# The second MoE in the order of the source on every queue, with z's sums on VectorE

## The chip, the core and the metric

The kernel runs on one core of a Trainium2 chip. The metric is the device time of one execution in microseconds (us), as the median of several runs. The engines are TensorE (PE; its weight loads are listed as PEld), VectorE (DVE), ScalarE (ACT), GpSimd (POOL) and SyncE (SP, which issues the DMAs here). The trace comes from one profiled execution.

## The reference, cut to what matters

```python
x = attention(q, k, v, mem_k, mem_v)      # 3072 tokens x 512, float32
h = np.maximum(x @ w_in, 0.0)             # first MoE: 512 -> 2048
x = (h * h) @ w_out                       # 2048 -> 512
g = x @ w_gate                            # second MoE: 512 -> 1536
val = x @ w_val
out = (g / (1 + np.exp(-g)) * val) @ w_out2    # 1536 -> 512
```

The second MoE takes gate and value as one 2x2 block product: the weights (A11, A12, A21, A22; 256 columns each) times the transposed tokens (B11, B21 of one block of 384 tokens, B12, B22 of the next), by a scheme with seven products in place of eight. It needs sums of the weights (S1 to S4, made once and kept in DRAM) and of the tokens: T1 = B12 - B11, T2 = B22 - B11, T3 = B22 - B12, T4 = T2 - B21. Every float32 factor is cut into a high part (a cast to float32r) and a low part (the rest), and a product is three passes over these parts.

## The kernel before, in words

Until 630 us of the profile the kernel does the attention and the first MoE. In the second MoE it takes the tokens in four groups `s` of two blocks and the 1536 columns in twelve slices `f`: 48 steps `i`, each with `gated(i)` (line 422) and then `output(i)` (line 463).

`gated` makes the seven products in two PSUM banks of `hbank`, p and q in turn, each with six matmuls (line 410: two halves of 128 rows, three passes). A product may start when the bank's last content, that of the product two earlier, has been read. The readers: ScalarE copies A11's product to p1 (line 426); VectorE adds S2's to p1 (u2, line 430), A12's to p1 (g0, line 434; ScalarE then takes its silu, line 435), S3's to u2 (u3, line 439), S1's to u3 and to u2 (c22 and u4, lines 443, 444), subtracts A22's from u3 (line 448) and multiplies by g0 (line 449), adds S4's to u4 (line 454); ScalarE takes u4's silu (line 455) and VectorE multiplies c22 by it (line 456). The two results are cut by `rounded` (line 416): ScalarE casts the high part uh (line 76), VectorE subtracts to get the low part ul (line 79).

`output(i)` is a generator of 18 matmuls of 512 columns from those parts into six banks, which sum over f. They run one step later, a few behind each product: `fill(1)`, `fill(3)` and so on. At the last f each bank is copied to a tile `o` by ScalarE or VectorE in turn and stored.

`side(1)` to `side(7)` stand behind the products and emit jobs for later steps: `load_gv` (a DMA of one half of a step's weights, 1024 or 768 columns, into one of the two tiles of "cut"), `split_gv` (ScalarE casts whi, POOL subtracts to get wlo, in two pieces), `load_out` and `split_out` (the same for the output weights of two steps), and for the next s, from f = 2 on, `load_z` (two DMAs of 768 KB, line 371), `split_b1`, `sums_1` and `sums_2` (the four T by POOL, lines 385 to 393) and `split_t` (ScalarE casts, VectorE subtracts, 128x768). Weights, output weights and the parts of the T share the 32 tiles of the pool `wp`.

What sets the order: TensorE follows the source from the second block of the first MoE on (`tc.manual_schedule`, line 560). The order of the other engines and of SP's DMAs is chosen at build time by a list scheduler, which goes by the order of the source as a priority and by when it takes data and buffers to be there. Each engine's queue is then worked off in that fixed order, so an instruction that waits holds up those behind it.

Of the kernel before, what the change touches and what calls it, by code (L numbers as in the profile page):

```python
# [7 lines left out]
F32 = mybir.dt.float32  # L8
# [3 lines left out]
ALU = mybir.AluOpType  # L12
# [17 lines left out]
NT2 = 384  # L30
# [17 lines left out]
def attention_moe_moe_kernel(ctx, tc, att, w1, w2, out):  # L48
# [9 lines left out]
    pe, act, dve, pool, sp = nc.tensor, nc.scalar, nc.vector, nc.gpsimd, nc.sync  # L58

    wp = ctx.enter_context(tc.tile_pool(name="wp", bufs=32))  # L60
# [13 lines left out]
    def split(hi, lo, src, hi_engine, lo_engine):  # L74
        if hi_engine is act:
            act.copy(hi, src)  # L76
        else:
            hi_engine.tensor_copy(hi, src)
        lo_engine.tensor_tensor(lo, src, hi.bitcast(F32), ALU.subtract)  # L79
# [150 lines left out]
    for t, n in enumerate(BLOCKS[1:], 1):  # L230
        for j in range(n):
            e = QB * (t - 1) + (j + 1) * QB // n - 15
# [4 lines left out]
    def attention(hs):  # L237
        for lag, fn, u in sorted(plan.pop(hs, []), key=lambda a: (-a[0], a[2])):
            fn(u)


    w = {}
# [3 lines left out]
    def pair(pool_, tag):  # L246
        return [pool_.tile([128, 1024], R, tag=tag, name=n) for n in ("whi", "wlo")]
# [61 lines left out]
    w2t = {}  # L309
# [24 lines left out]
        w["raw2", key] = raw[:, 0:n]  # L334
        sp.dma_start(out=raw[:, 0:n], in_=src)

    def split_w(key):
        raw = w.pop(("raw2", key))
        n = raw.shape[1]
        w2t[key] = pair(wp, "w")  # L340
        for c in (0, n // 2):
            split(*(t[:, c:c + n // 2] for t in w2t[key]), raw[:, c:c + n // 2], act, pool)

    def spare():
        return wp.tile([128, WC], F32, tag="w", name="spare")
# [5 lines left out]
        raw = rawp.tile([128, WC], F32, tag="cut", name="gvraw", bufs=CB)  # L351
        fetch((i, half), raw, w2g[seq2[i][1], :, c:c + NGV[half]], NGV[half])

    def split_gv(i, half):
        split_w((i, half))


    def load_out(i):
        fetch(("out", i), spare(), w2o[seq2[i][1] // 2], WC)

    def split_out(i):
        split_w(("out", i))

    zt, zraw = {}, {}

# [13 lines left out]
        hi, lo = zt[s][("B11", "B21")[k]] = [t[:, rows, 0:NT2] for t in zt[s]["x"]]  # L379
        split(hi, lo, zraw[s][0][:, rows], act, dve)  # L380

    def sums_1(s):
        z0, z1 = zraw[s]
        b11, b12, b22 = z0[:, 0:2], z1[:, 0:2], z1[:, 2:4]
        pool.tensor_tensor(b11, b12, b11, ALU.subtract)
        pool.tensor_tensor(b12, b22, b12, ALU.subtract)
        zt[s].update(T1=b11, T3=b12, B22=b22)

    def sums_2(s):
        z0, z1 = zraw[s]  # L390
        t2 = spare()[:, 0:2 * NT2].rearrange("p (k n) -> p k n", k=2)
        pool.tensor_tensor(t2, z1[:, 2:4], z0[:, 0:2], ALU.subtract)
        pool.tensor_tensor(z0[:, 2:4], t2, z0[:, 2:4], ALU.subtract)
        zt[s].update(T2=t2, T4=z0[:, 2:4])

    def split_t(s, name):
        src = zt[s][name]
# [3 lines left out]
    utile = {}  # L401

    def product(i, wname, zname, to):
        c = WAT[wname]
        whi, wlo = (t[:, c % WC:c % WC + QC] for t in w2t[i, c // WC])
        zh, zl = zt[seq2[i][0]][zname]
        n = 0
        for wt, z in ((whi, zh), (whi, zl), (wlo, zh)):
            for k in range(2):
                pe.matmul(to, wt[:, k * 128:k * 128 + 128], z[:, k], start=n == 0, stop=n == 5)  # L410
                n += 1

    def tmp():
        return up.tile([128, NT2], F32, tag="tmp", name="tmp", bufs=7)

    def rounded(u):
        uh = gp.tile([128, NTM], R, tag="gh", name="uh", bufs=3)[:, 0:NT2]
        ul = gp.tile([128, NTM], R, tag="gl", name="ul", bufs=3)[:, 0:NT2]
        split(uh, ul, u, act, dve)
        return uh, ul  # L420

    def gated(i, fill, side):
        p, q = (hbank[(7 * i + n) % 2][:, 0:NT2] for n in range(2))
        p1, u2, g0, u3, c22, u4 = (tmp() for _ in range(6))
        product(i, "A11", "B11", p)
        act.copy(p1, p)  # L426
        fill(1)
        side(1)
        product(i, "S2", "T2", q)
        dve.tensor_tensor(u2, q, p1, ALU.add)  # L430
        fill(3)
        side(2)
        product(i, "A12", "B21", p)
        dve.tensor_tensor(g0, p, p1, ALU.add)
        act.activation(g0, g0, AF.Silu)
        fill(3)
        side(3)
        product(i, "S3", "T3", q)
        dve.tensor_tensor(u3, q, u2, ALU.add)
        fill(3)  # L440
        side(4)
        product(i, "S1", "T1", p)
        dve.tensor_tensor(c22, p, u3, ALU.add)
        dve.tensor_tensor(u4, p, u2, ALU.add)
        fill(3)
        side(5)
        product(i, "A22", "T4", q)
        dve.tensor_tensor(u3, u3, q, ALU.subtract)
        dve.tensor_tensor(u3, u3, g0, ALU.mult)  # L449
        first = rounded(u3)  # L450
        fill(3)
        side(6)
        product(i, "S4", "B22", p)
        dve.tensor_tensor(u4, p, u4, ALU.add)  # L454
        act.activation(u4, u4, AF.Silu)
        dve.tensor_tensor(c22, c22, u4, ALU.mult)
        utile[i] = first, rounded(c22)
        fill(2)
        side(7)

    outs = [b[:, i] for i in range(2) for b in (yb0, yb1, abank)]

    def output(i):
        s, f = seq2[i]
        hi, lo = (t[:, f % 2 * DM:f % 2 * DM + DM] for t in w2t["out", i // 2 * 2])
        order = [(3 * b + j, p) for b in range(2) for p in range(3) for j in range(3)]
        if f == NF2 - 1:
            order = [(j, p) for j in range(6) for p in range(3)]
        for j, p in order:
            uh, ul = utile[i][j // 3]  # L470
            u, wt = ((uh, hi), (uh, lo), (ul, hi))[p]
            c = 128 * (j % 3)
            pe.matmul(outs[j], u[:, c:c + 128], wt, start=f == 0 and p == 0, stop=f == NF2 - 1 and p == 2)  # L473
            if f == NF2 - 1 and p == 2:
                o = up.tile([128, DM], F32, tag="o", name="o", bufs=3)
                if j % 2:
                    dve.tensor_copy(o, outs[j])
                else:
                    act.copy(o, outs[j])
                r0 = (6 * s + j) * 128  # L480
                sp.dma_start(out=out[r0:r0 + 128, :], in_=o)
            yield
# [16 lines left out]
    def at(hs, fn, *args):  # L499
        wplan.setdefault(hs, []).append((fn, args))  # L500
# [10 lines left out]
        at(a - 8, load2, c)  # L511
        at(a, prep2, c)
    for f, fn, *args in (
        (0, load_z, 0), (2, split_b1, 0, 0), (3, split_b1, 0, 1), (3, sums_1, 0), (4, sums_2, 0),
        (4, split_t, 0, "T2"), (5, split_t, 0, "T3"), (6, split_t, 0, "T1"), (6, load_gv, 0, 0), (7, split_t, 0, "T4"),
        (7, load_gv, 0, 1), (8, split_t, 0, "B22"), (9, load_out, 0), (9, split_gv, 0, 0), (10, split_gv, 0, 1),
        (11, load_gv, 1, 0), (12, split_out, 0), (12, load_gv, 1, 1), (13, split_gv, 1, 0), (14, split_gv, 1, 1),
        (14, load_out, 2),
    ):
        at(last + 4 * f + 2, fn, *args)  # L520
    lookahead = 2
# [2 lines left out]
    def side(hs):  # L524
        attention(hs)
        for fn, args in wplan.pop(hs, []):
            fn(*args)
# [29 lines left out]
    ordered = ExitStack()  # L557
# [22 lines left out]
    def job(i, slot, fn, *args):  # L580
        if i < len(seq2):
            jobs.setdefault((i, slot), []).append((fn, args))

    for i, (s, f) in enumerate(seq2):
        if i > 0:
            if i + 1 < len(seq2):
                job(i - 1, 4, load_gv, i + 1, 0)
                job(i - 1, 7, load_gv, i + 1, 1)
                job(i, 2, split_gv, i + 1, 0)
                job(i, 5, split_gv, i + 1, 1)  # L590
        if i % 2 == 0 and i + 2 < len(seq2):
            if i > 0:
                job(i, 7, load_out, i + 2)
            job(i + 1, 3, split_out, i + 2)
        if f == 0 and i + NF2 < len(seq2):
            for at_f, slot, fn, *args in (
                (2, 2, load_z), (4, 4, split_b1, 0), (5, 4, split_b1, 1), (6, 1, sums_1), (6, 4, sums_2),
                (7, 4, split_t, "T2"), (8, 4, split_t, "T3"), (9, 4, split_t, "T1"), (10, 4, split_t, "T4"),
                (11, 3, split_t, "B22"),
            ):  # L600
                job(i + at_f, slot, fn, s + 1, *args)
    todo = iter(())

    def fill(n):
        for _ in range(n):
            next(todo, None)

    for i in range(len(seq2)):
        def side2(slot):
            for fn, args in jobs.pop((i, slot), []):  # L610
                fn(*args)

        gated(i, fill, side2)
        todo = output(i)
    fill(18)
    ordered.close()
    uctx.close()
# [59 lines left out]
```

## Time and profile before

| | |
|---|---|
| median of 3 runs (lowest, highest) | 1245.71 us (1243.95, 1247.89) |
| the profiled execution, its span | 1246.47 us, 1244.7 us |
| TensorE busy in the span | 1168.9 us, 94% |
| VectorE, ScalarE, POOL busy | 718.2, 608.5, 376.1 us |
| second MoE, from its first product to its last matmul | 630.26 to 1240.39 us |

The span is that of the trace, from the first instruction to the last; the execution's own time is a little longer. TensorE is busy nearly all the time, so what can be gained without fewer matmuls is its idle time and the time in which its granted clock is low. In the rows, "idle before" names what ended an engine's wait, and "hbank L410" is a matmul of line 410.

### The profile page before, as it was taken

How to read it: one execution, taken by the hardware profiler on the slowest of the kernel's cores; microseconds unless marked ns; L12 is line 12 of the kernel's file. 1: busy time of each engine (PE TensorE's matmuls, PEld its weight loads, DVE VectorE, ACT ScalarE, POOL GpSimd, SP SyncE). 2: the span in 40 equal slices, each digit the busy share in tenths (PEclk: the TensorE clock that was granted, in tenths of full speed). 3: DMA queues.
4: the chain of work that ended last, by engine and by line, in shares of the span. 5: the costliest groups of instructions: out<-in, count | busy, mean ns of one | idle time of the engine just before them, and what ended most of it. 6: DMA issues, size and time to landing. Idle time of an engine off the chain costs nothing.

```text
span 1244.7 us, 20548 instructions
## 1 busy us (share of the span) xinstructions
PE 1168.9 (94%) x8000; PEld 1101.3 (88%) x8000; DVE 718.2 (58%) x1223; ACT 608.5 (49%) x1518; POOL 376.1 (30%) x313
## 2 busy tenths in 40 slices
PE   2699999999999999999989999899998999989998
PEld 1599999999999999999978999789987899878897
DVE  7997335546454464533356666566665666555654
ACT  5686545556455564545643344544344343443422
POOL 0000000202020020002565445754367543564610
PEclk9999999999999999999989999899999999989999
DMA  7553205527243451501353224522245232353301
GB/s 266 192 207 116 74 25 177 185 87 253 82 161 131 166 197 61 207 1 51 103 167 100 77 73 145 178 88 85 93 123 183 77 95 68 113 165 98 93 13 51
DMA packets 49441, 150.22 MB, mean 121 GB/s; under 512 B 4800, under 2 KB 14528, under 8 KB 44992
## 3 DMA queue, kind: packets, MB, share of 16 engines
q1 hardware_dynamic: 49344, 148.92, 36.0%
q8 instruction: 62, 1.02, 0.3%
q14 instruction: 35, 0.29, 0.1%
HBM read 122.16 MB, written 26.74 MB: 120 GB/s over the span
## 4 chain that ended last, share of the span: by engine, by line
PE 78%; DVE 8%; DMA 5%; POOL 3%; ACT 2%; issue 2%; SPq 0%; DVEq 0%; POOLq 0%; ACTq 0%
PE hbank L410 24%; PE yb L295 19%; PE hbank L264 19%; PE yb L473 9%; PE abank L473 4%; POOL wlo L79 3%; DMA wraw<-in_w_dram 3%; PE abank L197 2%; DMA gvraw<-w2g 2%; DVE pT L178 2%; PE abank L136 1%; DVE tmp L449 1%; DVE ul L79 1%; DVE cut L97 1%; ACT uh L76 1%
## 5 line engine op out<-in xcount | busy, mean ns | idle before, releaser
L79 POOL TENSOR_TENSOR wlo<-gvraw,whi 128x512 fp32r<-128x512 f32 x192 | 233.7, 1239 | 247.4 <-ACT whi L76 122.7
L264 PE MATMUL hbank<-x,whi 128*128 128x384 f32 x1024 | 200.3, 337 | 1.0 <-ACT x L76 0.6
L274 DVE TENSOR_TENSOR gl<-r,gh 128x384 fp32r<-128x384 f32 x128 | 79.2, 620 | 182.8 <-ACT r L273 182.3
L264 PEld LDWEIGHTS hbank<-x,whi 128*128 128x128 f32 x1024 | 180.4, 189 | 1.8 <-ACT x L76 0.9
L328 POOL TENSOR_TENSOR wraw<-cut 128x256 f32<-128x256 f32 x24 | 19.8, 847 | 462.6 <-DVE mx L149 343.8
L410 PE MATMUL hbank<-whi 128*128 128x384 f32 x480 | 126.5, 345 | 19.9 <-DVE tmp L454 13.8
L76 ACT CAST whi<-gvraw 128x512 fp32r<-128x512 f32 x192 | 100.5, 563 | 86.3 <-DMA gvraw<-w2g 38.6
L271 ACT ACTIVATE r<-hbank 128x384 f32<-128x384 f32 x128 | 62.9, 491 | 143.5 <-PE hbank L264 140.6
L410 PEld LDWEIGHTS hbank<-whi 128*128 128x128 f32 x480 | 89.2, 190 | 47.0 <-DVE tmp L454 20.0
L76 ACT CAST uh<-tmp 128x384 fp32r<-128x384 f32 x96 | 49.3, 514 | 161.7 <-DVE tmp L449 124.2
L410 PE MATMUL hbank<-wlo,whi 128*128 128x384 f32 x480 | 126.3, 344 | 0.0
L410 PE MATMUL hbank<-whi,wlo 128*128 128x384 f32 x480 | 124.7, 341 | 0.0
L295 PE MATMUL yb<-gh,whi 128*128 128x384 f32 x512 | 116.3, 341 | 0.0
L295 PE MATMUL yb<-gh,wlo 128*128 128x384 f32 x512 | 113.4, 335 | 0.0
L295 PE MATMUL yb<-gl,whi 128*128 128x384 f32 x512 | 113.3, 335 | 0.0
L264 PE MATMUL hbank<-x,wlo 128*128 128x384 f32 x512 | 109.8, 335 | 0.0
L79 DVE TENSOR_TENSOR ul<-tmp,uh 128x384 fp32r<-128x384 f32 x96 | 77.4, 806 | 48.2 <-ACT uh L76 46.0
L178 DVE STREAM_TRANSPOSE pT<-prob 32x256 f32<-32x256 f32 x224 | 97.3, 434 | 3.6
L410 PE MATMUL hbank<-z,whi 128*128 128x384 f32 x384 | 86.1, 347 | 5.8 <-ACT tmp L426 5.8
L295 PEld LDWEIGHTS yb<-gh,whi 128*128 128x128 f32 x512 | 89.2, 188 | 2.5
L295 PEld LDWEIGHTS yb<-gh,wlo 128*128 128x128 f32 x512 | 91.4, 188 | 0.0
L295 PEld LDWEIGHTS yb<-gl,whi 128*128 128x128 f32 x512 | 90.9, 188 | 0.1
(91 smaller groups left out, 2132.9 us busy)
## 6 DMA issues: line engine op xcount, KB each, us to landing
wraw<-in_w_dram SPq DMA_DIRECT2D x34, 1024.0 KB, 6.6
gvraw<-w2g SPq DMA_DIRECT2D x48, 512.0 KB, 3.5
gvraw<-w2g SPq DMA_DIRECT2D x48, 384.0 KB, 3.1
qk<-in_att_dram SPq DMA_DIRECT2D x32, 464.0 KB, 4.5
spare<-w2o SPq DMA_DIRECT2D x24, 512.0 KB, 3.3
v<-in_att_dram SPq DMA_DIRECT2D x32, 256.0 KB, 3.5
y1d<-ys SPq DMA_DIRECT2D x8, 768.0 KB, 3.8
w2g<-wraw SPq DMA_DIRECT2D x12, 512.0 KB, 4.0
```

What stands on the lines that cost most here:

```text
L76: act.copy(hi, src)
L79: lo_engine.tensor_tensor(lo, src, hi.bitcast(F32), ALU.subtract)
L97: dve.scalar_tensor_tensor(w.bitcast(I32), upper, 3, lower, ALU.logical_shift_left, ALU.bitwise_or)
L178: dve.transpose(pT[row:row + 32, :, 32 * c:32 * c + 32], probs[u % 2][32 * c:32 * c + 32, :, col:col + 32],)
L197: pe.matmul(o[r:r + D, h // NI, h % NI // 2], s["v"][:, h * D:(h + 1) * D], pT[:, h], start=True, stop=True, tile_position=(0, r),)
L264: pe.matmul(hps, wt[:, k * 128:(k + 1) * 128], x[:, k, 0:n], start=i == 0, stop=i == 3 * KD - 1)
L271: act.activation(r, hps, AF.Relu)
L274: dve.tensor_tensor(gl, r, gh.bitcast(F32), ALU.subtract)
L295: pe.matmul(y[e], wt[:, c:c + 128], g, start=f == 0 and p == 0, stop=f == NF1 - 1 and p == 2)
L328: pool.tensor_tensor(o, x, y, op)
L410: pe.matmul(to, wt[:, k * 128:k * 128 + 128], z[:, k], start=n == 0, stop=n == 5)
L473: pe.matmul(outs[j], u[:, c:c + 128], wt, start=f == 0 and p == 0, stop=f == NF2 - 1 and p == 2)
```

## The change

All engines and SP's DMA queue now follow the source in the second MoE, as TensorE did already, and the source is put in another order: behind each product its reader comes first, then `side`, then `fill`. The cut of u's halves is divided: `halves_of` emits the cast on ScalarE and `low_of` the subtraction on VectorE. The first half's subtraction comes behind u4's addition; the second half's cast comes at the end of the step and its subtraction behind the next step's u2 (`pending`). `split_gv` and `split_out` are divided into two parts with slots of their own. The four sums of z go from POOL to VectorE, one at a time.

```diff
+    def sum_t(s, name):
+        z0, z1 = zraw[s]
+        b11, b12, b21, b22 = z0[:, 0:2], z1[:, 0:2], z0[:, 2:4], z1[:, 2:4]
...
+        o, x, y = {"T1": (b11, b12, b11), "T3": (b12, b22, b12), "T2": (t2, b22, b11), "T4": (b21, t2, b21)}[name]
+        dve.tensor_tensor(o, x, y, ALU.subtract)
...
-    def rounded(u):
+    def halves_of(u):
...
-        split(uh, ul, u, act, dve)
+        act.copy(uh, u)
+        return uh, ul, u
+
+    def low_of(uh, ul, u):
+        dve.tensor_tensor(ul, u, uh.bitcast(F32), ALU.subtract)
         return uh, ul
+    pending = []
...
         product(i, "A11", "B11", p)
         act.copy(p1, p)
+        side(1)
         fill(1)
-        side(1)
         product(i, "S2", "T2", q)
         dve.tensor_tensor(u2, q, p1, ALU.add)
+        if pending:
+            low_of(*pending.pop())
+        side(2)
         fill(3)
-        side(2)
...
         dve.tensor_tensor(u3, u3, q, ALU.subtract)
         dve.tensor_tensor(u3, u3, g0, ALU.mult)
-        first = rounded(u3)
+        side(6)
+        first = halves_of(u3)
         fill(3)
-        side(6)
         product(i, "S4", "B22", p)
         dve.tensor_tensor(u4, p, u4, ALU.add)
+        utile[i] = [low_of(*first)]
         act.activation(u4, u4, AF.Silu)
         dve.tensor_tensor(c22, c22, u4, ALU.mult)
-        utile[i] = first, rounded(c22)
         fill(2)
         side(7)
+        second = halves_of(c22)
+        pending.append(second)
+        utile[i].append(second[0:2])
...
-                job(i, 2, split_gv, i + 1, 0)
-                job(i, 5, split_gv, i + 1, 1)
+                for slot, half, part in ((1, 0, 0), (2, 0, 1), (4, 1, 0), (5, 1, 1)):
+                    job(i, slot, split_gv, i + 1, half, part)
...
-            job(i + 1, 3, split_out, i + 2)
+            job(i + 1, 3, split_out, i + 2, 0)
+            job(i + 1, 6, split_out, i + 2, 1)
...
-                (2, 2, load_z), (4, 4, split_b1, 0), (5, 4, split_b1, 1), (6, 1, sums_1), (6, 4, sums_2),
-                (7, 4, split_t, "T2"), (8, 4, split_t, "T3"), (9, 4, split_t, "T1"), (10, 4, split_t, "T4"),
-                (11, 3, split_t, "B22"),
+                (2, 1, load_z), (4, 4, split_b1, 0), (5, 4, split_b1, 1), (5, 7, sum_t, "T1"), (6, 2, sum_t, "T3"),
+                (6, 4, sum_t, "T2"), (6, 7, sum_t, "T4"), (7, 4, split_t, "T2"), (8, 4, split_t, "T3"),
+                (9, 4, split_t, "T1"), (10, 4, split_t, "T4"), (11, 4, split_t, "B22"),
...
+    ordered.enter_context(tc.manual_schedule(engines={e.engine for e in (act, dve, pool, sp)}))
     for i in range(len(seq2)):
```

In the last block of the first MoE, where the first s is prepared, the same functions are called in two parts at the same places, and the sums T1 and T3, T2 and T4 where `sums_1` and `sums_2` stood. At the end of the kernel the last pending subtraction comes ahead of the last output matmuls.

## Rows read from the trace of the kernel before

**Rows 1.** Windows: the four groups s, an undisturbed step, the step opening s = 1.
```profile
core 0: us, PE busy (x) PEld busy (x) DVE busy (x) ACT busy (x) POOL busy (x), PEclk, DMA share, GB/s
630.26:777.28 147.02, 139.34 (x704) 127.89 (x703) 93.60 (x139) 60.47 (x119) 75.10 (x56) 0.98 0.36 113
777.28:928.84 151.56, 143.86 (x722) 131.06 (x720) 93.49 (x142) 65.42 (x130) 83.83 (x65) 0.98 0.37 114
928.84:1082.37 153.53, 143.41 (x722) 130.37 (x721) 92.48 (x141) 64.15 (x128) 81.50 (x65) 0.99 0.34 104
1082.37:1240.39 158.02, 149.06 (x739) 134.47 (x737) 88.89 (x141) 58.31 (x119) 63.02 (x51) 0.98 0.27 86
905.00:916.60 11.60, 11.60 (x62) 10.80 (x60) 6.55 (x13) 4.24 (x9) 2.53 (x2) 1.00 0.30 93
777.28:797.07 19.79, 14.67 (x61) 12.78 (x60) 8.13 (x14) 10.23 (x21) 15.67 (x14) 0.83 0.56 180
```

**Rows 2.** Chain of waits, 905 to 917 us: start, us, what.
```profile
908.20 1.06 PE hbank L410 x6
```

**Rows 3.** Waits of TensorE, 630 to 1245 us: us in total, times, longest.
```profile
PE hbank L410 <- DVE tmp L454: 13.8, 17, 1.5
PE yb L473 <- ACT uh L76: 6.3, 6, 1.5
PE hbank L410 <- DVE tmp L444: 5.9, 3, 5.3
PE hbank L410 <- ACT tmp L426: 5.8, 3, 3.7
```

**Rows 4.** Timeline of VectorE, 664 to 673 us: start, us, what, idle before.
```profile
667.88 1.60 DVE L449 TENSOR_TENSOR tmp<-tmp 128x384 f32<-128x384 f32 x1
670.06 0.99 DVE L79 TENSOR_TENSOR ul<-tmp,uh 128x384 fp32r<-128x384 f32 x1 [0.58 <-ACT uh L76]
670.98 0.55 DVE L454 TENSOR_TENSOR tmp<-hbank,tmp 128x384 f32<-128x384 f32 x1
```

**Rows 5.** Timeline of all engines, 900 to 930 us: the end of one step.
```profile
901.22 0.56 DVE L443 TENSOR_TENSOR tmp<-hbank,tmp 128x384 f32<-128x384 f32 x1 [1.20 <-PE hbank L410]
...
902.98 0.56 DVE L448 TENSOR_TENSOR tmp<-tmp,hbank 128x384 f32<-128x384 f32 x1 [0.74 <-PE hbank L410]
...
905.25 0.55 DVE L454 TENSOR_TENSOR tmp<-hbank,tmp 128x384 f32<-128x384 f32 x1
...
905.89 0.52 ACT L455 ACTIVATE tmp<-tmp 128x384 f32<-128x384 f32 x1
...
906.33 0.46 ACT L426 COPY tmp<-hbank 128x384 f32<-128x384 f32 x1
906.45 0.56 DVE L456 TENSOR_TENSOR tmp<-tmp 128x384 f32<-128x384 f32 x1 [0.65 <-ACT tmp L455]
...
907.04 0.51 ACT L76 CAST uh<-tmp 128x384 fp32r<-128x384 f32 x1 [0.26 <-DVE tmp L456]
...
907.80 0.77 PEld L410 LDWEIGHTS hbank<-z,whi 128*128 128x128 f32 x4
```

**Rows 6.** Timeline of ScalarE, 777 to 791 us.
```profile
784.78 0.51 ACT L76 CAST whi<-gvraw 128x384 fp32r<-128x384 f32 x1 [4.42 <-DMA gvraw<-w2g]
785.20 0.52 ACT L455 ACTIVATE tmp<-tmp 128x384 f32<-128x384 f32 x1
785.62 0.46 ACT L426 COPY tmp<-hbank 128x384 f32<-128x384 f32 x1
```

**Rows 7.** Timeline of POOL, 899 to 919 us.
```profile
910.90 2.53 POOL L79 TENSOR_TENSOR wlo<-gvraw,whi 128x512 fp32r<-128x512 f32 x2 [9.13 <-PE hbank L410]
916.72 2.87 POOL L79 TENSOR_TENSOR wlo<-spare,whi 128x512 fp32r<-128x512 f32 x2 [3.29 <-ACT whi L76]
```

**Rows 8.** Timelines: one sum of z on POOL; one T split on VectorE.
```profile
773.83 2.55 POOL L385 TENSOR_TENSOR zraw<-zraw 128x768 f32<-128x768 f32 x1
...
915.11 0.96 DVE L79 TENSOR_TENSOR wlo<-zraw,whi 128x768 fp32r<-128x768 f32 x1
```

**Rows 9.** The page's DMA issues: count, KB each, median us to landing.
```profile
gvraw<-w2g SPq DMA_DIRECT2D x48, 512.0 KB, 3.5
```

More of the change, by code (lines that the diff above doesn't have):

```diff
@@ L335, in fetch, with split_w @@
         sp.dma_start(out=raw[:, 0:n], in_=src)
[L337 to L342, printed above, removed]
+    def split_w(key, part):
+        raw = w["raw2", key]
+        n = raw.shape[1] // 2
+        if part == 0:
+            w2t[key] = pair(wp, "w")
+        c = slice(n * part, n * part + n)
+        split(*(t[:, c] for t in w2t[key]), raw[:, c], act, pool)
     def spare():
@@ L352, in load_gv, with split_gv, split_out @@
         fetch((i, half), raw, w2g[seq2[i][1], :, c:c + NGV[half]], NGV[half])
-    def split_gv(i, half):
-        split_w((i, half))
+    def split_gv(i, half, part):
+        split_w((i, half), part)
     def load_out(i):
         fetch(("out", i), spare(), w2o[seq2[i][1] // 2], WC)
-    def split_out(i):
-        split_w(("out", i))
+    def split_out(i, part):
+        split_w(("out", i), part)
     zt, zraw = {}, {}
@@ L380, in split_b1 @@
         split(hi, lo, zraw[s][0][:, rows], act, dve)
-    def sums_1(s):
+    def sum_t(s, name):
         z0, z1 = zraw[s]
[L384 to L394, printed above, removed]
+        b11, b12, b21, b22 = z0[:, 0:2], z1[:, 0:2], z0[:, 2:4], z1[:, 2:4]
+        t2 = zt[s].get("T2")
+        if name == "T2":
+            t2 = spare()[:, 0:2 * NT2].rearrange("p (k n) -> p k n", k=2)
+        o, x, y = {"T1": (b11, b12, b11), "T3": (b12, b22, b12), "T2": (t2, b22, b11), "T4": (b21, t2, b21)}[name]
+        dve.tensor_tensor(o, x, y, ALU.subtract)
+        zt[s][name] = o
+        zt[s]["B22"] = b22
     def split_t(s, name):
@@ L435, in gated @@
         act.activation(g0, g0, AF.Silu)
+        side(3)
         fill(3)
-        side(3)
         product(i, "S3", "T3", q)
         dve.tensor_tensor(u3, q, u2, ALU.add)
+        side(4)
         fill(3)
-        side(4)
         product(i, "S1", "T1", p)
@@ L444, in gated @@
         dve.tensor_tensor(u4, p, u2, ALU.add)
+        side(5)
         fill(3)
-        side(5)
         product(i, "A22", "T4", q)
@@ L513, in attention_moe_moe_kernel @@
     for f, fn, *args in (
[L514 to L518, printed above, removed]
+        (0, load_z, 0), (2, split_b1, 0, 0), (3, split_b1, 0, 1), (3, sum_t, 0, "T1"), (3, sum_t, 0, "T3"),
+        (4, sum_t, 0, "T2"), (4, sum_t, 0, "T4"), (4, split_t, 0, "T2"), (5, split_t, 0, "T3"), (6, split_t, 0, "T1"),
+        (6, load_gv, 0, 0), (7, split_t, 0, "T4"), (7, load_gv, 0, 1), (8, split_t, 0, "B22"), (9, load_out, 0),
+        (9, split_gv, 0, 0, 0), (9, split_gv, 0, 0, 1), (10, split_gv, 0, 1, 0), (10, split_gv, 0, 1, 1),
+        (11, load_gv, 1, 0), (12, split_out, 0, 0), (12, split_out, 0, 1), (12, load_gv, 1, 1), (13, split_gv, 1, 0, 0),
+        (13, split_gv, 1, 0, 1), (14, split_gv, 1, 1, 0), (14, split_gv, 1, 1, 1), (14, load_out, 2),
     ):
@@ L614, in attention_moe_moe_kernel @@
         todo = output(i)
+    low_of(*pending.pop())
     fill(18)
```

## The prediction

> **What bounds the kernel now.** I read the windows by stretch first. The second MoE begins with the first product of line 410 at 630.26 us and fills the rest of the span: 48 steps, cut in the windows into four stretches of twelve by s [rows 1]. A step without any wait takes 11.60 us, and TensorE is busy in all of it [rows 1]; seven products of six matmuls at 1.06 us each [rows 2] are 7.42 of that, and the 18 output matmuls of the step before are the other 4.18. Nothing in the change touches a matmul, so 11.60 is the floor of a step. Against it stand: s = 0, 147.02 us for one step without output work (7.42) and eleven full ones (127.60), 12.0 too much; s = 1, 151.56 against 139.20, 12.4; s = 2, 153.53 against 139.20, 14.3; s = 3, 158.02 against 139.20 and the 4.18 of the last output, 14.6. **53.3 us** are lost in all, and that is all that an order of the work can win back here.
>
> Then the waits of TensorE alone [rows 3]: four rows make 31.8 us of idle time, and none names a weight or a DMA. 13.8 us go to u4's addition at line 454, 17 times, the others to line 444, to the copy of p1 (line 426) and to uh's cast. All are readers of a PSUM bank or a cast behind one: they come late because something else stands ahead of them on VectorE or ScalarE. The other 21.5 us are small waits, the restart after each and time at half clock: the step that opens s = 1 takes 19.79 us and shows a mean granted clock of 0.83 [rows 1], 2.4 GHz with a part at 1.2 after the waits.
>
> Two pictures of it. On VectorE, the timeline at 667 to 671 us shows u3's product (line 449) at 1.60 us where its like at line 456 takes 0.56, then ul, which waited for ScalarE, and only then line 454 [rows 4, 5]; the source has the rounding of u3 ahead of it. On ScalarE, at 780 us, a cast of gvraw waits 4.42 us for its DMA, and the silu of line 455 and p1's copy, whose inputs are there, stand behind it [rows 6]. The scheduler put them there; TensorE waits for both.
>
> **Part by part.**
>
> *Readers first, other work behind* (fill after side, `low_of` and `halves_of` in place of `rounded`). Line 454's addition no longer stands behind ul. Its product, S4, can be read 1.76 us after A22 (readers of successive products start at 901.22 and 902.98 [rows 5]), so at 904.74 in that step, while the addition ran at 905.25. The 13.8 us go.
>
> What is late next: u's second half. Its cast now stands ahead of the next step's p1 copy on ScalarE, and the cast waits for VectorE's multiplication. From the addition at R: silu at R + 0.64, product at R + 1.20, uh's cast at R + 1.79 (905.25, 905.89, 906.45, 907.04 [rows 5]); p1's copy 0.44 behind the cast as it is behind the silu, and 0.46 long: done at R + 2.69. ul of the first half, put between addition and product, takes VectorE from R + 0.47 to R + 1.03 and so fits into the time of the silu. With R = 904.74 p1 is there at 907.43; TensorE loads A12's first weights at 907.80 [rows 5]. So 0.37 us are left: price 0, with that cover. If the cover goes, each 0.1 us beyond it is paid in 47 steps.
>
> POOL could take that cover. In steps with even f it has the four halves of gv: 2.53 us for the first two [rows 7] and, by their columns, three quarters of it for the others; in odd ones another 2.87 for out [rows 7]. Split by halves into slots 1, 2, 4, 5 (and 3, 6), the casts run right behind p1 and the first silu, so POOL works from about 3 to 8 us of a step (to 11 in odd ones) and rests at its end, where the chain is. Lower bound of a stall 0, upper one below as a rival.
>
> *The order of the source on ACT, DVE, POOL and SP.* The work for the next s (loads of z, B1 and T splits, sums) now runs where the source puts it, f = 2 to 11, not in step 0 or in the last step as now. Step 0 then waits for no z: 13.8 us now (7.42 with no wait), and I take 8.2, since without output work u4's addition still holds up S4 a little. That T splits cost TensorE nothing where they stand behind a reader is to be seen: one of 0.96 us lies in the step 905.00 to 916.60, which took 11.60 [rows 1, 8].
> ScalarE's queue now blocks for good where a DMA is late. Half 0 of gv is free when POOL is done with it, some 5.8 us into a step; 3.5 us to land [rows 9] make 9.3, and the cast comes at 11.6 + 2.3. Half 1: about 9.5 in an odd step, landed by 13, cast at 16.9. Some 4 us of margin each, so 0. The 32 tiles of wp hold this order: at most 18 for T (T2 is free after S2 of f = 11), 8 for gv, 4 for out and a raw one, 31; so no cast waits for a tile, or rows 6 would come back. On SP, load_z moves from slot 2 to slot 1, past nothing but the next gv load; its buffers came free at f = 11 of the step before: 0. At f = 0 the six stores of the output stand in SP's queue ahead of load_out and load_gv, the last behind line 456; those two then land about 6.3 us into f = 1, a microsecond after the cast wants them, POOL ends late and meets u3's product: between 0 and 0.7 us of stall (1.04 as in rows 4 less 0.37), I take 0.4, three times: 1.2.
>
> *z's sums on VectorE.* Four per s leave POOL (2.55 us for one [rows 8]) and come to VectorE, which does 128x768 in 0.96 us [rows 8]. POOL's time is off the path: worth 0 by itself. T1, T2 and T4 stand where the next reader has room: 0. T3 stands in slot 2 behind u2 and ul, and g0's reader comes 1.76 us after u2's: 0.55 + 0.56 + 0.96 is 0.3 too much, and that reader may be 1.4 late before S1 waits for its bank (two products of 1.76, less 1.06, the 0.2 until a reader starts, its 0.6 and the early load of weights, 0.23). If both VectorE operations meet POOL there, 2 x 1.04 come on top and S1 waits about 1.0. gv's half 0 is on POOL just then, so I take the 1.0: three times, 3.0.
> What the rows show is 1.60 us for a two-operand VectorE operation that began 0.1 us behind one of POOL's. The Trainium skill (SBUF — State Buffer, Who interferes with whom) says that such an operation and a GpSimd one that reads SBUF share one read port as an exclusive lock: whichever comes second blocks for the whole of the other. The trace agrees (1.60 against 0.56); without the lock T3 would cost 0 and the sum be 3.0 us lower, and the rule speaks against moving sums to an engine that POOL blocks.
>
> *The sum.* Left of the 53.3: step 0, 0.8; T3, 3.0; f = 1, 1.2; the last output 1.0, as now. 53.3 - 6.0 = 47.3 us. The profiled execution took 1246.47 us (span 1244.7 and 1.8 around it), 0.8 above the median of 1245.71: 1246.47 - 47.3 - 0.8 = **1198.4**. The first MoE ends as before; four sums join VectorE's list in its last block, where no attention is left: 0. With nothing left but floors it would be 1192.
>
> **Rivals.**
>
> *A wait at the end of every step.* ScalarE has uh's second cast ahead of p1's copy, and the product before that cast has two SBUF operands. For it: pieces of POOL's meet such products now, as rows 4 show; against it: the order by slots leaves POOL idle there. If an operation of POOL's is under way in each step, the product takes 1.04 longer, 0.67 beyond the cover: 47 x 0.67 = 31.5 us, 1230 us. If ul meets one as well, another 0.43 (0.99 in rows 4 against 0.56): 47 x 1.10 = 51.7 us, 1250, **slower than before**. It turns at 47.3 / 47, a stall of 1.0 us per step. A small stall of 0.1 to 0.5 gives 1203 to 1222.
>
> *VectorE loses more time to POOL.* A split of z in slot 4 that finds one operation of POOL's under way (1.27 us [rows 7]) takes 2.23 us with its own 0.96; with u3's addition ahead of it, c22's reader is 0.9 late, and S4 has 0.96 of room (two products of 1.76 less 1.06, 0.2, 0.23 and the two readers' 1.07). Two in a row make 2.2 late: 1.25 us of stall, and 12 sums and 21 splits run in this stage. All of them: 41 us, 1239; half: 1219. Against it: the step with a T split took 11.60 [rows 1, 8]. It is the lock that the Trainium skill describes (SBUF — State Buffer, Who interferes with whom), at its worst.
>
> *The DMA wait stays in ScalarE's queue.* Order by source does not make gvraw land sooner. If loads still come late at the three changes of s, the waits there stay, about half of what is won: 1224. For it: rows 6; against: no z work at that time any more.
>
> *The order does not hold* (TensorE's own order is let go by the new scope, or the scheduler had the same order anyway): about 1246. Against it: rows 6 show an order that is not the source's.
>
> **How the numbers follow.** Forecast (1192 to 1206): 0.66. A small stall in each step: 0.12. DMA or lock keep part: 0.09. Order without effect: 0.05. End-of-step wait at full size: 0.08, half of it slower. A measurement of this kernel tells about 0.3%, 3.7 us, from no change. Faster: 0.66 + 0.12 + 0.09 and a part of the 0.08: 0.89. Same: 0.05. Slower: 0.06. Range: from the floor, 1192, to a stall of 0.5 us in every step, 1224, which holds the forecast, the small stall and half of the third: 0.8.
>
> **What would show it.** Right: twelve steps of s = 1 within 142 us; line 454 no longer among TensorE's waits; granted clock 1.00 to the end; z's casts spread over f = 4 to 11; step 0 near 8 us. T3: a wait of about 1 us at f = 6 for g0's addition. Wrong: TensorE waiting for p1's copy in most steps, with POOL's wlo under way at the multiplication of c22; or ScalarE waiting for gvraw with p1's copy behind it.

## The result: 1195.51 us, and the profile after

| | before | after |
|---|---|---|
| median (lowest, highest), 4 runs each | 1246.06 us (1243.95, 1247.89) | 1195.51 us (1194.18, 1195.91) |
| the profiled execution, its span | 1246.47, 1244.7 us | 1195.23, 1193.5 us |
| TensorE busy in the span | 1168.9 us, 94% | 1150.7 us, 96% |
| second MoE, first product to last matmul | 610.13 us | 558.26 us |

The ratio is 0.9593, with a 95% interval from 0.9576 to 0.961: faster by 50.6 us, where 1198.4 was forecast. The windows of the four groups s, as [rows 1], and then the one long step:

```profile
core 0: us, PE busy (x) PEld busy (x) DVE busy (x) ACT busy (x) POOL busy (x), PEclk, DMA share, GB/s
630.14:765.36 135.22, 135.15 (x704) 125.95 (x703) 85.50 (x142) 60.35 (x121) 74.48 (x56) 1.00 0.34 110
765.36:904.56 139.20, 139.20 (x722) 129.52 (x720) 89.23 (x148) 64.94 (x130) 79.67 (x60) 1.00 0.38 125
904.56:1043.76 139.20, 139.20 (x722) 129.55 (x720) 89.22 (x148) 64.94 (x130) 79.61 (x60) 1.00 0.38 125
1043.76:1188.40 144.64, 144.28 (x739) 132.44 (x737) 77.70 (x142) 59.56 (x122) 66.35 (x54) 1.00 0.30 99
1066.96:1078.99 12.03, 11.88 (x62) 10.73 (x61) 6.86 (x12) 4.32 (x9) 6.25 (x6) 1.00 0.45 152
```

Against the floors (135.02, 139.20, 139.20 and 143.38 with the last output) 0.2, 0, 0 and 1.3 us are left: 1.5 of the 53.3. The stretch of s = 1 and that of s = 2 have TensorE busy from end to end, and the granted clock is 1.00 where s = 1 had 0.98 [rows 1]. The engines' work has hardly changed (VectorE 89.23 against 93.49 us in s = 1, ScalarE 64.94 against 65.42): it stands elsewhere. VectorE's time fell although it took over the four sums, since fewer of its operations meet one of POOL's: of its operations of 128x384 in this stage 93 took over 0.7 us in before and 17 do in after, all of them with both operands in SBUF (all operations of that size together: 351.6 us before, 309.9 after). TensorE's waits in the second MoE, as [rows 3], are these two rows and no others:

```profile
PE yb L483 <- DVE ul L422: 0.2, 1, 0.2
PE hbank L409 <- ACT tmp L431: 0.2, 1, 0.2
```

The 31.8 us of the four rows of before are gone. What stood behind a part of them was ScalarE's wait for the weights' DMA [rows 6]. That row of ScalarE's waits in the second MoE, before and then after:

```profile
ACT whi L76 <- DMA gvraw<-w2g: 37.8, 16, 4.4
...
ACT whi L76 <- DMA gvraw<-w2g: 2.5, 3, 2.0
```

Of the three that are left only one leads to a loss (f = 1, below).

A part of the 53.3 us was clock. In before TensorE's granted clock stood at its lower level, 1.2 GHz, in four stretches (from 641, 784, 952 and 1102 us, 24 us together), each begun within or just behind a wait of TensorE; one of them, its clock column at 0.51 (windows of before):

```profile
784.30:791.30 7.00, 5.17 (x15) 4.88 (x16) 3.74 (x5) 4.19 (x9) 6.15 (x6) 0.51 0.51 161
```

TensorE was busy in 20 of these 24 us, at half its clock, so some 10 us were lost to it (an estimate), about half of the 21.5 us that the prediction left to small waits, restarts and the clock. In after the granted clock stays at the higher level up to the last matmul.

The end of a step, on VectorE, then ScalarE, then the weight loads (three timelines, 891 to 896 us):

```profile
892.70 0.56 DVE L461 TENSOR_TENSOR tmp<-hbank,tmp 128x384 f32<-128x384 f32 x1 [0.61 <-PE hbank L409]
893.17 0.55 DVE L422 TENSOR_TENSOR ul<-tmp,uh 128x384 fp32r<-128x384 f32 x1
893.91 0.56 DVE L464 TENSOR_TENSOR tmp<-tmp 128x384 f32<-128x384 f32 x1 [0.19 <-ACT tmp L463]
...
894.56 0.52 ACT L418 CAST uh<-tmp 128x384 fp32r<-128x384 f32 x1 [0.68 <-DVE tmp L464]
894.98 0.47 ACT L431 COPY tmp<-hbank 128x384 f32<-128x384 f32 x1
...
895.76 0.77 PEld L409 LDWEIGHTS hbank<-z,whi 128*128 128x128 f32 x4
```

u4's addition (line 461) starts at R = 892.70, p1's copy (line 431) ends at 895.45, R + 2.75, and TensorE loads A12's weights at 895.76: the copy is 0.31 us early, where the prediction worked out 0.37. The kernel lives on that cover in 47 steps, so the experiments go for it, and for which engine's order counts.

### The profile page after: what moved, and what is told of

Same layout as the page of the kernel before. It is cut to its first block, busy times and chain, and to the rows that moved or that the text cites. A ratio compares the mean times of both kernels' runs of the same rounds, so it can differ in the third digit from the quotient of the medians.

```text
span 1193.5 us, 20592 instructions
## 1 busy us (share of the span) xinstructions
PE 1150.7 (96%) x8000; PEld 1094.5 (92%) x8000; DVE 692.2 (58%) x1239; ACT 605.2 (51%) x1518; POOL 355.4 (30%) x297
## 4 chain that ended last, share of the span: by engine, by line
PE 89%; DVE 6%; DMA 2%; ACT 1%; issue 1%; SPq 0%; ACTq 0%; DVEq 0%
PE hbank L409 30%; PE yb L295 20%; PE hbank L264 20%; PE yb L483 11%; PE abank L483 6%; PE abank L197 2%; DVE pT L178 2%; DMA wraw<-in_w_dram 2%; PE abank L136 1%; DVE cut L97 1%; ACT prob L157 1%; DVE wlo L79 0%; DVE prob L173 0%; DVE wraw L95 0%; DMA qk<-in_att_dram 0%
## 5 line engine op out<-in xcount | busy, mean ns | idle before, releaser
L79 POOL TENSOR_TENSOR wlo<-gvraw,whi 128x512 fp32r<-128x512 f32 x192 | 252.2, 1333 | 296.5 <-ACT whi L76 224.9
L409 PE MATMUL hbank<-whi 128*128 128x384 f32 x480 | 122.5, 337 | 0.1
L264 PEld LDWEIGHTS hbank<-x,wlo 128*128 128x128 f32 x512 | 90.7, 188 | 0.0
L157 ACT ACTIVATE prob<-abank,mx 96x72 f32<-96x72 f32 x224 | 68.3, 318 | 40.5 <-DVE mx L149 40.5
```

The lines of the kernel that those rows point to most:

```text
L157: act.activation(probs[u % 2][:, h, 0:WK], s["s"][:, r, i], AF.Exp, bias=s["mx"][:, r, i:i + 1], scale=SCALE, accum_out=s["sm"][:, h],)
L264: pe.matmul(hps, wt[:, k * 128:(k + 1) * 128], x[:, k, 0:n], start=i == 0, stop=i == 3 * KD - 1)
```

## The experiments

Times are medians; "on top" is against after's 1195.51 us. The kernel before, measured again beside the experiments, had medians from 1244.07 to 1247.25 us, so a difference between kernels that were not measured side by side can be some 3 us off. The profiled executions begin the second MoE anywhere from 627.8 to 634.4 us, whatever was edited behind that point, so an edit worth less than 5 us is read from the lengths of its steps.

**1. No order held.** The source of after without the new scope:

```diff
-    ordered.enter_context(tc.manual_schedule(engines={e.engine for e in (act, dve, pool, sp)}))
```

> The changed source, but the new scope that holds ScalarE, VectorE, POOL and SP to it is taken out, so the list scheduler orders them again. If the held order is what wins, the scheduler brings z's casts and gv's casts forward again and the waits at the changes of s come back: about 30 of the 51 us are lost, 1215 to 1240 us; line 461's addition may still come in time, since the source has it ahead of ul. Rival, the new places in the source are enough as priorities: within 5 us of the changed kernel, 1195 to 1200 us.

1240.63 us, ratio to before 0.9952 (0.9933 to 0.9972): just beyond the far end of what was expected. Without the scope the new source is worth 6.6 us against the 1247.25 of before measured beside it. TensorE's waits and a stretch of ScalarE at the change from s = 0 to s = 1:

```profile
PE hbank L409 <- DVE tmp L461: 13.3, 15, 1.6
PE yb L483 <- ACT uh L418: 10.1, 8, 2.8
```

```profile
784.90 0.93 ACT L76 CAST whi<-gvraw 128x384 fp32r<-128x384 f32 x2 [2.60 <-DMA gvraw<-w2g]
788.75 1.14 ACT L76 CAST whi<-gvraw 128x512 fp32r<-128x512 f32 x2 [2.92 <-DMA gvraw<-w2g]
...
790.27 0.51 ACT L418 CAST uh<-tmp 128x384 fp32r<-128x384 f32 x1
```

It is [rows 6] over again: casts for a later step wait for their DMA, and uh's cast stands behind them. Line 461's addition did not come in time either: its row of 13.3 us is that of before, and on VectorE ul stands ahead of it again (790.81 against 792.28 us), though the source has it the other way.

**2. The scope alone.** The source of before, with that one line added ahead of its last loop.

> The kernel before with the new scope alone: its own source order held on all queues. The waits for gvraw and zraw ahead of p1's copy should go (z's work then runs at f = 2 to 11). But u4's addition stands behind ul of the first half, which waits for ScalarE: R comes about 0.6 us late, and the chain to p1's copy, which has 0.3 to 0.37 us of cover, then ends 0.2 to 0.6 us late in every step: 47 times, 10 to 28 us, 1205 to 1223 us in all. Rival, holding any sensible order is enough: 1195 to 1200 us. Other rival, the old order held is as bad as the scheduler's: above 1240 us.

1214.57 us, 0.9756 (0.9718 to 0.9793): 32.7 us off before, 19.1 on top of after. As expected. So the hold is the larger part, and it needs no new source for that. In it TensorE waits 1.7 us for u4's addition, against 13.8 [rows 3], though ul still stands ahead of it (two of the four rows of its waits):

```profile
PE hbank L410 <- ACT tmp L426: 2.9, 12, 0.4
PE hbank L410 <- DVE tmp L454: 1.7, 5, 0.6
```

**3 and 4. One engine held.** After, with `(act,)` or with `(dve,)` in place of `(act, dve, pool, sp)` in the scope.

> After's kernel with the order of the source held on ScalarE alone; VectorE, GpSimd and the DMA queue are left to the scheduler. My theory: what costs most without any hold is that casts of gv stand in ScalarE's queue ahead of uh's cast, the silu and p1's copy, and wait there for their DMA (8.6 us of such waits from 765 to 806 us in the run with no hold, in which the two steps at the change of s lost 8.7). With ScalarE in order these go, and what stays is TensorE's wait for u4's addition behind ul on VectorE (13.3 us, 15 times, in that run): 1206 to 1220 us, the steps 0 and 1 of s = 1 at 11.6 to 12.5 each. Rival: the orders count only together, since a DMA that the scheduler issues late now blocks ScalarE for good: 1225 to 1245, with the steps at the change of s still at 14 to 19.

> After's kernel with the order of the source held on VectorE alone. My theory: the wait for u4's addition (13.3 us) goes nearly whole, while the casts that wait for gv's DMA ahead of uh's cast on ScalarE stay, so steps 0 and 1 of s = 1 still take 13 to 18 us: 1215 to 1232. Rival: VectorE's order is what counts, ScalarE's casts come in good time by themselves: 1195 to 1208.

ScalarE alone: 1211.97 us, 0.9743 (0.9727 to 0.976). VectorE alone: 1221.65, 0.9824 (0.9802 to 0.9847). Both inside what my theory gave. Against experiment 1 the one is worth 28.7 us, the other 19.0; together 47.7, where holding all four is worth 45.1. In the profiled executions, where the second MoE takes 601.8 us with no order held, 576.2 with ScalarE's, 585.7 with VectorE's and 558.3 in after, it is 25.6 and 16.1, together 41.7 of 43.5. So the two parts add up as well as these runs can tell. What holding POOL and SP adds was not run by itself; by these sums it can be a few us at most. The low clock goes with the long waits: 17 us of the second MoE stand at 1.2 GHz with no order held and as many with VectorE's, none with ScalarE's. With VectorE held, ScalarE's row on the DMA is still there, and so are steps of 17.9 us; with ScalarE held the row is gone, and TensorE's waits are small ones (VectorE held, ScalarE's and TensorE's waits; then ScalarE held, TensorE's):

```profile
ACT whi L76 <- DMA gvraw<-w2g: 39.4, 22, 2.9
...
PE yb L483 <- ACT uh L418: 9.8, 5, 3.3
```

```profile
PE hbank L409 <- DVE tmp L461: 3.2, 12, 0.3
PE hbank L409 <- ACT tmp L431: 2.8, 14, 0.7
```

In the second I had expected the 13.3 us for line 461 to stay whole; the row shows 3.2, while the time is where I expected it. The next experiment shows why both hold.

**5. ul first.** After, with one pair of lines in the old order:

```diff
-        dve.tensor_tensor(u4, p, u4, ALU.add)
         utile[i] = [low_of(*first)]
+        dve.tensor_tensor(u4, p, u4, ALU.add)
```

> After's kernel with one thing put back: the low half of u's first half (ul) stands ahead of u4's addition on VectorE, as in the source of before; everything else as in after. The old order with the engines held lost some 19 us against after, of which 6 are the sums on GpSimd (the run that moves them alone). My theory: most of the other 13 is this one place. Where the scheduler put ul first with ScalarE alone held, u4's addition began 0.45 us behind the time at which it could (756.59 against 754.38 + 1.76 = 756.14), which is beyond the 0.3 of cover, and such steps took 12.55: 0.2 to 0.9 us in 47 steps where ul is in the way, 1206 to 1222, with TensorE waiting for line 461 and for p1's copy. Rival: the 13 come from the places of the casts and of the output matmuls (halves of a split in slots of their own, output behind the reader): then 1195 to 1201, steps of 11.60.

1209.28 us, 0.971 (0.9674 to 0.9747): 13.8 on top, the 13 that were looked for (14.8 by the second MoE of the profiled execution). Every second step takes some 12.1 us (windows of two neighbours, f = 6 and 7 of s = 3), and yet the waits of TensorE, in the second fence, are small:

```profile
1130.24:1142.37 12.13, 11.95 (x62) 10.63 (x60) 6.08 (x12) 4.48 (x10) 4.81 (x4) 1.00 0.36 130
1142.37:1154.07 11.70, 11.70 (x62) 10.70 (x60) 6.08 (x11) 5.17 (x11) 7.28 (x6) 1.00 0.22 61
```

```profile
PE hbank L409 <- ACT tmp L431: 4.3, 24, 0.2
PE yb L483 <- ACT o L489: 0.9, 1, 0.9
PE hbank L409 <- DVE tmp L462: 0.2, 1, 0.2
```

5.4 us of waits stand for 13.8 us of time. One such wait, in TensorE's timeline:

```profile
1133.13 0.40 PE L483 MATMUL yb<-wlo,uh 128*128 128x512 f32 x1
1133.71 0.97 PE L409 MATMUL hbank<-z,whi 128*128 128x384 f32 x4 [0.18 <-ACT tmp L431]
```

and the same place in after:

```profile
1128.19 0.40 PE L483 MATMUL yb<-wlo,uh 128*128 128x512 f32 x1
1128.42 0.87 PE L409 MATMUL hbank<-z,whi 128*128 128x384 f32 x4
```

In after the product starts 0.23 us behind the matmul ahead of it and overlaps its 0.40; here it starts 0.58 behind. That is 0.35 lost, of which the profile calls 0.18 idle, since it counts from the modelled end of the matmul before. The four matmuls then take 0.97 instead of 0.87. Together 0.45, nearly the 0.43 by which this step is longer than its neighbour. Short waits of TensorE are read from the starts, not from the waits.

**6. The sums on POOL.** After, with one word changed:

```diff
-        dve.tensor_tensor(o, x, y, ALU.subtract)
+        pool.tensor_tensor(o, x, y, ALU.subtract)
```

> The changed kernel with z's four sums back on POOL, at the new places. If the order of the queues is what won the time, the sums' engine is worth nothing: POOL rests about 4 us of each step and no sum's result is wanted for a step. Second MoE still 11.60 us per step, 1193 to 1198 us. Rival, POOL was what made the weights late at the changes of s: POOL gets about 8.5 us more work in f = 5 to 7 of each s, its wlo come late, steps 6 to 8 of each s show waits, 1205 to 1226 us.

1201.26 us, 0.9655 (0.9624 to 0.9687): 5.8 on top, between what the two theories gave. So the prediction's step "worth 0 by itself" failed, by 5.8 us. Two steps in each of the three groups are longer, f = 6 and f = 7 (windows). As each begins, a sum on POOL (line 391) is under way while VectorE does the end of the step before: the first time ul meets it (first fence of timelines, VectorE and POOL), the second time the multiplication of c22 (second fence, VectorE, POOL, ScalarE):

```profile
699.98:712.29 12.31, 11.85 (x61) 10.70 (x60) 7.59 (x13) 4.53 (x10) 9.85 (x7) 1.00 0.25 84
712.29:725.17 12.88, 11.88 (x61) 10.72 (x60) 9.27 (x13) 6.40 (x13) 10.89 (x8) 1.00 0.32 102
```

```profile
700.60 1.54 DVE L422 TENSOR_TENSOR ul<-tmp,uh 128x384 fp32r<-128x384 f32 x1
...
699.56 2.16 POOL L391 TENSOR_TENSOR zraw<-zraw 128x768 f32<-128x768 f32 x1
```

```profile
713.27 2.20 DVE L464 TENSOR_TENSOR tmp<-tmp 128x384 f32<-128x384 f32 x1
...
712.89 2.16 POOL L391 TENSOR_TENSOR zraw<-spare,zraw 128x768 f32<-128x768 f32 x1
...
715.55 0.51 ACT L418 CAST uh<-tmp 128x384 fp32r<-128x384 f32 x1 [2.35 <-DVE tmp L464]
715.97 0.47 ACT L431 COPY tmp<-hbank 128x384 f32<-128x384 f32 x1
```

0.71 and 1.28 us, three times: 6.0. ul takes 1.54 instead of 0.55, the multiplication 2.20 instead of 0.56, so uh's cast and p1's copy are late. That is the first rival's mechanism, in 6 steps of 48; with the sums on VectorE, POOL is not under way in that place. With experiment 5 it makes 13.8 + 5.8 = 19.6, and 19.1 is what the old source loses with everything held; that the other moves in the source are worth next to nothing follows from this sum alone, none of them was run by itself.

**7 and 8. The cover at the end of a step.** After, with one and with two more operations ahead of the multiplication of c22; the one line, and the same line twice:

```diff
         act.activation(u4, u4, AF.Silu)
+        dve.tensor_tensor(g0, u3, u2, ALU.add)
         dve.tensor_tensor(c22, c22, u4, ALU.mult)
```

> After's kernel with one more VectorE operation of 128x384 between u4's addition and the multiplication of c22, so that the multiplication starts some 0.1 to 0.2 us later (it starts 0.56 behind the silu's start now and VectorE then rests only until the silu ends; two such operations lost 0.39 us in each full step). My theory: the cover at the end of a step is 0.3 us, so this stays inside it: steps of 11.60, 0 to 3 us on top of after, 1195 to 1199. Rival: there is no cover, a step already ends on p1's copy and each 0.1 us later is paid: 0.1 to 0.2 us in 47 steps, 1200 to 1206, steps of 11.70 to 11.80.

> The changed kernel with two more additions on VectorE (0.56 us each, result unused) in each step between ul of the first half and the multiplication of c22, so this product comes about 0.67 us later. The cover ahead of A12's weight load is 0.3 to 0.37 us by the trace, so 0.3 to 0.4 us of stall per step (a little more in odd steps, where the chain already starts 0.2 us late): 14 to 25 us on top, 1209 to 1220 us, with TensorE waiting for p1's copy in each step. Rival, the end-of-step chain is not near the path and VectorE has time to spare: under 3 us.

The added sums go into g0, which nothing reads any more. Two: 1217.01 us, 0.9773 (0.9737 to 0.9808), 21.5 on top. All full steps but seven take 11.97 to 12.01 (the seven, six of them at f = 1 and 2, take 12.06 to 13.45), as this one:

```profile
876.11:888.10 11.99, 11.87 (x61) 10.71 (x60) 8.28 (x15) 6.09 (x12) 8.12 (x6) 1.00 0.19 55
```

One: 1200.75 us, 0.9654 (0.9633 to 0.9676), 5.2 on top, where the theory said 0 to 3 and the rival 0.1 to 0.2 us in every step. Neither holds. The odd steps but two keep 11.60, and there p1's copy now ends 0.12 us ahead of the weight load instead of 0.31: the cover exists, and the operation takes 0.19 of it. But 14 of the 23 full even steps take 11.89 to 12.47: f = 6, 8, 10 and the next f = 0 nearly always, f = 2 behind each change of s, and none of the last four, in whose group no z is cut. Except at f = 2 their chain is late from the odd step before on, as here at the end of f = 5 (timelines of VectorE and ScalarE):

```profile
697.45 1.57 DVE L456 TENSOR_TENSOR tmp<-tmp 128x384 f32<-128x384 f32 x1
698.94 0.55 DVE L461 TENSOR_TENSOR tmp<-hbank,tmp 128x384 f32<-128x384 f32 x1
...
701.18 0.52 ACT L418 CAST uh<-tmp 128x384 fp32r<-128x384 f32 x1 [1.08 <-DVE tmp L465]
701.61 0.47 ACT L431 COPY tmp<-hbank 128x384 f32<-128x384 f32 x1
```

In odd steps POOL also has the cuts of out, a cut of z makes it later still, and its last piece is under way when u3's multiplication (line 456) comes: 1.57 instead of 0.56, and line 461 starts late. The same place in after (timelines of ScalarE and the weight loads):

```profile
697.98 0.48 ACT L431 COPY tmp<-hbank 128x384 f32<-128x384 f32 x1
...
698.56 0.77 PEld L409 LDWEIGHTS hbank<-z,whi 128*128 128x128 f32 x4
```

The copy ends at 698.46: 0.10 us of cover are left there, against 0.31 at 895 us. In after it is 0.06 to 0.12 in all twelve steps of this kind. Less 0.19 that is some 0.1 us too little, and the steps lose about 0.3: a stall costs more than the time by which p1's copy is late, as in experiment 5.

**9. Two sums in one slot.** After, with the sum T1 beside T3:

```diff
-                (2, 1, load_z), (4, 4, split_b1, 0), (5, 4, split_b1, 1), (5, 7, sum_t, "T1"), (6, 2, sum_t, "T3"),
+                (2, 1, load_z), (4, 4, split_b1, 0), (5, 4, split_b1, 1), (6, 2, sum_t, "T1"), (6, 2, sum_t, "T3"),
```

> After's kernel with the sum T1 moved from slot 7 of f = 5 into slot 2 of f = 6, ahead of T3, so that two sums stand between u2's and g0's readers. My theory: there g0's reader may be 1.43 us late before TensorE waits and is 1.34 late now behind T3 alone; a second sum of 0.95 to 2.05 us makes it 2.3 to 3.4 late, and the step f = 6 of s = 0, 1 and 2 loses 0.9 to 2.0 us each: 2.7 to 6 us in all, 1198 to 1202, with TensorE waiting for line 441 or for the lines behind it. Rival: the room there is larger than I worked out (that it cost nothing in after says only that): step f = 6 stays at 11.60 and the time at 1194 to 1197.

1201.29 us, 0.9653 (0.9638 to 0.9669): 5.8 on top. Step f = 6 takes 13.32 us instead of 11.60 in three groups, 5.2 in all: as expected. The two sums take 4.01 us, and TensorE waits for line 441, which stands behind them (VectorE's timeline, then TensorE's waits):

```profile
697.79 4.01 DVE L391 TENSOR_TENSOR zraw<-zraw 128x768 f32<-128x768 f32 x2
```

```profile
PE hbank L409 <- DVE tmp L441: 4.4, 3, 1.5
```

Line 441 starts at 701.72, 3.3 us later than in an undisturbed step of after, and the step loses 1.7, so the room there is about 1.6 us. The prediction worked out 1.4, and T3 alone fits into that.

## Why the prediction was right, point by point

**What bounds, and the floor.** Right: 51.9 us of the 53.3 came back (610.13 to 558.26), all of it in the second MoE, and the steps stand at 11.60. The profiled execution fell by 51.2, and the tail behind the last matmul grew by 0.8 (1244.7 - 1240.39 = 4.3 before, 1193.5 - 1188.40 = 5.1 after).

**Readers first.** Right in sum, with half of the cause. "The 13.8 us go" because line 454 no longer stands behind ul, said the prediction. But in before ul also stands ahead of it in steps that lose nothing, and makes it 0.5 us late there (905.25 against 904.74 [rows 5]). In 16 of the 17 waits of [rows 3] u3's product took 1.0 to 1.6 us or ul 1.3 to 1.9 instead of 0.56, each with an operation of POOL's under way as it began; [rows 4] show one such place. In four of the 17, at the changes of s, uh's cast was late as well. So two things came together, ul in front and POOL beside it, and it is enough to take one away: with ul behind and POOL left to the scheduler TensorE has no such wait (experiment 4), with ul in front and the queues held the row falls to 1.7 (experiment 2), as POOL's pieces then mostly miss these operations. With everything held, ul in front still costs 13.8 us, but by another way (experiment 5): p1's copy is then the last link, and a step has 0.3 us to spare. The two numbers agree by chance.

**The cover.** 0.37 forecast, 0.31 read where POOL rests, and experiments 7 and 8 bear it out there. That POOL "rests at its end" (of a step) fails in the odd steps that also cut z: it reaches into u3's multiplication, and about 0.1 us is left. In after that costs nothing, as something is left; 0.19 us more was paid for in these steps (experiment 7), and at some 0.3 us a step, where the prediction has "each 0.1 us beyond it" paid as it is.

**Order of the source.** Right: step 0 took 7.63 us (8.2 forecast, so 0.8 lost; it lost 0.2), and the DMA wait in ScalarE's queue fell to 2.5 us. Experiment 4 shows what the prediction gained by that: with ScalarE's queue left to the scheduler, 39.4 us of such waits come back. The PSUM page of the Trainium skill (PSUM — Partial Sum Buffer, Engine vs sequencer instructions) has the queues of ScalarE, VectorE and GpSimd as strict first in, first out; the rows of experiment 1 show what that costs when the head of ScalarE's waits.

**f = 1.** The mechanism is right but for the operation that POOL meets, which is ul and not u3's product; the term of 1.2 is too large. In s = 3 alone the loads came late enough: ScalarE's cast waited 1.95 us for gvraw, POOL's pieces ran on into the end of the step, and ul met one (VectorE and POOL of after):

```profile
1067.17 1.64 DVE L422 TENSOR_TENSOR ul<-tmp,uh 128x384 fp32r<-128x384 f32 x1
...
1067.10 1.29 POOL L79 TENSOR_TENSOR wlo<-spare,whi 128x512 fp32r<-128x512 f32 x1
```

That is the step of 12.03 us: 0.43, as sized (0.4), but once and not three times. It is the same step in experiments 6 and 9 (11.89 and 12.21 us); why only s = 3 has it stays open.

**z's sums.** Two steps failed here, and they point to opposite sides. T3 was put at 3.0 and cost 0: "if both VectorE operations meet POOL" was taken as the case, and only the sum met it, not ul (VectorE and then POOL of after):

```profile
698.96 0.55 DVE L422 TENSOR_TENSOR ul<-tmp,uh 128x384 fp32r<-128x384 f32 x1
699.43 2.05 DVE L391 TENSOR_TENSOR zraw<-zraw 128x768 f32<-128x768 f32 x1
701.40 0.55 DVE L441 TENSOR_TENSOR tmp<-hbank,tmp 128x384 f32<-128x384 f32 x1
...
699.05 3.59 POOL L79 TENSOR_TENSOR wlo<-gvraw,whi 128x512 fp32r<-128x512 f32 x2 [3.68 <-ACT whi L76]
```

The sum takes 2.05 instead of 0.95 (0.96 for as many elements in [rows 8]). ul had begun 0.09 us ahead of POOL's pieces and took its 0.55, in all three groups alike; which of the two comes first was nowhere worked out in the prediction. Line 441 begins 1.50 behind A12's weight load in an undisturbed step (897.26 behind 895.76), so here it was due at 698.56 + 1.50 = 700.06 and is 1.34 late: just inside the 1.4 that the prediction gave it. And "POOL's time is off the path: worth 0 by itself" was wrong: freeing POOL of the sums is worth 5.8 us once its splits stand in the order of the source (experiment 6), because POOL holds up VectorE's operations that have both operands in SBUF. The rule of the Trainium skill that I weighed (SBUF — State Buffer, Who interferes with whom) holds in its rows: 2.20 for c22's multiplication that began 0.38 us behind a sum of POOL's lasting 2.16. I read it as speaking against sums on VectorE; it speaks more strongly against sums on POOL.

**The sum.** Left of 53.3: step 0, 0.2 (0.8 forecast); T3, 0 (3.0); f = 1, 0.4 (1.2); the last output 0.8 (1.0): 1.5 where 6.0 was forecast. The step on the median (0.8 off) did not apply, as after's profiled execution lies 0.3 below its median, and the tail took 0.8. 4.5 - 0.8 - 1.1 are 2.6 of the 2.9 us between 1198.4 and 1195.51. The range's upper end, 1224, belongs to a stall of 0.54 us in every step, not of 0.5 (1222); nothing hangs on it.

**The rivals.** None happened in after. The wait at the end of every step is one or two operations away (experiments 6 to 8). Splits of z do meet POOL (1.42 us instead of 0.95 at 899.65 us), and their steps keep 11.60. The DMA wait in ScalarE's queue is what the kernel has without that queue's order (39.4 us, experiment 4). That the order does not hold is excluded by the rows; experiment 1, where it doesn't, gives 1240.63, near the 1246 that was put on it.

## What to carry to other kernels

Where one engine is the bound and the others only feed it, look in the queues for work for later steps that stands ahead of a reader: fixing their order was worth 26 to 29 us here in ScalarE's queue and 16 to 19 in VectorE's, where moving one operation within that order was worth 5.8 to 13.8. Work out the chain at the end of a step against the next weight load, and test the cover with one more operation before more work is put there. An engine that holds up VectorE's operations with both operands in SBUF (POOL here) isn't off the path only because nobody waits for its results: see which operation it meets.

## What the runs showed of the hardware that I had not expected

A wait of TensorE costs more than its row: 5.4 us of rows for 13.8 us of time in experiment 5 (start to start 0.58 instead of 0.23, idle 0.18).

What meets POOL depends on where the operands lie. At 701.40 us of after line 441, with one operand in PSUM, took its 0.55 us while POOL's two pieces (699.05, 3.59 us) were still under way; the sum just ahead of it, with both in SBUF, took 2.05 instead of 0.95.

After and experiments 5 and 7 to 9 have the same source ahead of the second MoE, and yet it begins anywhere from 628.3 to 634.2 us in their profiled executions. In two of them TensorE's early wait for qk's DMA differs (9.7 us where it begins at 633.0, 6.9 where it begins at 628.5); the cause stays open.
